# Unit 8's k transposed by VectorE and an HBM round trip, with new engine sequences, in an RWKV and ELU-MLP kernel on one Trainium2 core

## Chip, core and metric

The kernel runs on one core of one Trainium2 chip. The metric is the device time of one execution in microseconds (us), the median of several runs. All times below come from those runs or from one profiled execution of the same kernel.

## The reference, cut to what matters

```
B, H, S, D = 4, 8, 768, 48
state = zeros(B, H, D, D)
for t in range(S):
    cur = einsum('bhd,bhe->bhde', u * k[t], v[t])
    y[t] = einsum('bhd,bhde->bhe', r[t], state + cur)
    state = w[t][..., None] * state + einsum('bhd,bhe->bhde', k[t], v[t])
x = y as (B*S, H*D) = (3072, 384)
h = x @ w_in                        # 384 -> 2048
g = where(h > 0, h, exp(min(h, 0)) - 1)
out = g @ w_out                     # 2048 -> 384
```

A linear recurrence over 768 steps with a decay per channel (RWKV) feeds a two-layer perceptron with an ELU between its layers. All data are float32.

## The kernel before

**Work.** The recurrence is computed in chunks. There are 24 units: units 0 to 3 are one batch each over the first 128 steps, every later unit is two batches over 64 steps. Four units give the 512 columns of one of six blocks of the perceptron (c = 0 to 5). Each block runs over 16 slices of the hidden layer. A float32 product is made of three TensorE passes (w_h by x_h, w_h by x_l, w_l by x_h), so one slice is nine multiplications of 128x128 by 512 columns in layer one (`g1`, line 267) and nine in layer two (`g2`, line 298). Block 0 has 23 pieces (n = 0 to 22), since its columns are taken in halves at first, and each later block 16, so pieces go to n = 102.

**Steps of a unit i.** On VectorE (DVE): `es` and `gs` (decay products by scans, lines 461 and 470/471), `rkc` and then `rh` (k and r scaled, 495 and 476), `mk` (the upper triangle of the scores is put into the tile `ams`, 599 to 605), `sc` and `up` (the state, 632 and 698), `xl` (the low part of x, 690). On ScalarE (ACT): `md` (the diagonal, 504), `sp` (the diagonal spread into `ams`, 518, eight instructions for units 0 to 7; later units spread on GpSimd by an affine select, 529), `kt` (609), `xh` (686). On TensorE (PE): `pd` (500), `s` (scores, 570), `va` (for units from 8: the next unit's scores and this unit's state update, 570 and 640), `v` (values, 550). `mk` of unit i needs `s` and `sp` of unit i, `v` needs `mk`.

**Steps of a piece n.** g1 (PE), `r1` and `r2` (ACT, 271 and 274), `stt` (DVE, 277), `gh` (ACT, 281), `gl` (DVE, 285), g2 (PE). There are two PSUM buffers for g1's result, so g1 of n waits for `stt` of n - 2.

**Weights.** Every slice f is loaded raw (`raw`, 227), made float on ACT (`a`, 231) and DVE (`cc`, 235), split (`wh` on ACT, `wl` on DVE, 731), and its largest value is taken (`big`, DVE, 734), which is used at the end alone. Slices 0 and 1 are split later: `wt` (ACT), `wl` (DVE) and `wh` on GpSimd (POOL, line 727).

**The transpose of k.** `va` needs k with time on the partitions. For units 0 to 8 TensorE transposes (line 563, within `s`; for unit 8 a step of its own, `tr`), and ACT copies the result from PSUM (`kt`). For the units in TURN (9 to 21) VectorE transposes blocks of 32x32 (`tn`, 618), four DMAs write them to HBM in another order (`tw`, 623), and one DMA reads them back (`tk`, 627). Then the k load of the unit takes 128 rows, not 112.

**What sets the order.** Each of the five queues has its order written out in a table (SEQUENCE); each engine takes its steps strictly in that order. All loads, stores and copies are on one queue, that of SyncE (SP). A planner with a table of costs (COST) merges the five orders into one program text; within an engine it changes nothing. FILL puts warm-up multiplications by a matrix of ones (line 426) ahead of the named PE steps at the start; one call is two multiplications in the trace.

Of the kernel before, what the change touches and what calls it, by code (L numbers as in the profile page):

```python
# [85 lines left out]
g2.37 g2.38 g1.41 g1.42 g2.39 va.13 v.13 g2.40 g1.43 g2.41 g1.44 g1.45 g2.42 g2.43 g1.46 va.14 v.14 g1.47 g2.44 g2.45 g1.48 g1.49 va.15 v.15 g2.46
g1.50 g2.47 g2.48 g1.51 g1.52 g2.49 g2.50 g1.53 g1.54 va.16 v.16 g2.51 g1.55 g2.52 g1.56 g2.53 g2.54 va.17 v.17 g1.57 g1.58 g2.55 g1.59 g2.56 g2.57
va.18 v.18 g1.60 g1.61 g2.58 g1.62 g1.63 g2.59 g2.60 g1.64 g2.61 va.19 v.19 g1.65 g2.62 g1.66 g2.63 g1.67 g2.64 g1.68 g2.65 g1.69 g2.66 g1.70 g2.67
va.20 v.20 g1.71 g2.68 g1.72 g2.69 g2.70 g1.73 g1.74 g2.71 g1.75 g1.76 g2.72 g2.73 g2.74 va.21 v.21 g1.77 g2.75 g1.78 g1.79 g2.76 g1.80 va.22 v.22
# [5 lines left out]
es.0 gs.0 rkc.0 es.1 rh.0 gs.1 rkc.1 mk.0 rh.1 cc.0 es.2 rkc.2 gs.2 mk.1 rh.2 cc.1 es.3 stt.0 gs.3 cc.2 xl.0 stt.1 xl.1 wl.2 cc.3 rkc.3 stt.2 mk.2
rh.3 stt.3 wl.3 cc.4 es.4 es.5 gl.3 wl.4 cc.5 mk.3 stt.4 wl.5 stt.5 rk.4 gl.4 big.3 cc.6 stt.6 gs.4 gl.5 xl.3 gl.6 xl.2 rku.4 stt.7 md.4 stt.8 cc.7
wl.6 rh.4 stt.9 sc.4 rk.5 gl.9 cc.8 gs.5 rku.5 stt.10 md.5 stt.11 rh.5 wl.7 mk.4 wl.8 gl.11 gl.10 cc.9 sc.5 rk.6 stt.12 stt.13 xl.4 es.6 up.4 rku.6
gl.13 gl.12 cc.10 gs.6 mk.5 stt.14 wl.9 gl.14 rh.6 cc.11 stt.15 md.6 wl.10 rk.7 wl.11 cc.12 gl.15 stt.16 up.5 xl.5 rku.7 es.7 sc.6 cc.13 stt.17 wl.12
gl.16 mk.6 md.7 cc.14 gs.7 gl.17 sc.7 stt.18 rh.7 wl.13 stt.19 up.6 wl.14 es.9 gl.18 xl.6 cc.15 stt.20 es.8 gl.19 wl.15 rk.8 mk.7 sc.8 stt.21 gs.9
gl.20 gl.21 rk.9 rku.8 xl.7 gs.8 rku.9 rh.8 stt.22 md.8 md.9 rh.9 gl.22 up.7 stt.23 tn.9 es.10 rk.10 gl.23 sc.9 stt.24 gs.10 rh.10 gl.24 stt.25 tn.10  # L100
es.11 rk.11 gl.25 rku.11 mk.8 big.10 stt.27 stt.26 md.11 rku.10 md.10 up.8 gs.11 gl.27 gl.26 mk.9 sc.10 rh.11 es.12 stt.28 big.11 rk.12 gl.28 xl.8
stt.29 gs.12 big.2 stt.30 up.9 tn.11 mk.10 gl.29 sc.11 rh.12 stt.31 xl.9 es.13 gl.30 gl.31 wl.1 wl.0 rku.12 gs.13 md.12 es.14 rk.13 stt.32 gl.32
rku.13 up.10 stt.33 gs.14 gl.33 tn.12 stt.34 sc.12 rk.14 rh.13 xl.10 stt.35 mk.11 gl.34 md.13 rku.14 gl.35 es.15 big.9 tn.13 stt.36 mk.12 rh.14 gl.36
up.11 xl.11 stt.37 gs.15 md.14 es.16 rk.15 stt.38 sc.13 rku.15 gs.16 gl.38 gl.37 mk.13 md.15 tn.14 rh.15 up.12 stt.39 rk.16 stt.40 xl.12 gl.39 rku.16
tn.15 gl.40 stt.41 md.16 rh.16 es.18 gl.41 gs.18 up.13 stt.42 sc.14 stt.43 gl.42 es.17 gs.17 gl.43 tn.16 stt.44 big.12 mk.14 sc.15 big.14 stt.45 gl.44
xl.13 rk.17 rh.17 rku.17 gl.45 es.19 stt.46 mk.15 big.13 up.14 xl.14 big.6 tn.17 stt.47 big.0 gs.19 md.17 gl.46 rk.18 stt.48 gl.47 sc.16 rh.18 stt.49
gl.48 xl.15 es.20 tn.18 up.15 rku.18 stt.50 mk.16 md.18 rh.19 gl.49 sc.17 gl.50 rk.19 stt.51 stt.52 gl.51 gs.20 gl.52 rk.20 tn.19 rku.19 big.15 stt.53
md.19 es.21 gs.21 stt.54 up.16 gl.53 gl.54 big.5 big.4 mk.17 sc.18 rku.20 stt.56 xl.16 stt.55 mk.18 gl.55 gl.56 rh.20 big.8 rk.21 tn.20 rku.21 stt.57
stt.58 xl.17 rh.21 es.22 gl.57 es.23 up.17 stt.59 gl.58 up.18 gs.23 sc.19 md.20 gl.59 tn.21 md.21 stt.60 rk.22 stt.61 gl.60 stt.62 gs.22 big.7 gl.61
mk.19 rku.22 stt.63 xl.18 md.22 gl.62 rk.23 stt.64 rku.23 gl.63 md.23 stt.65 up.19 rh.22 sc.21 gl.64 sc.20 gl.65 stt.66 stt.67 xl.19 mk.20 gl.66 gl.67  # L110
big.1 stt.68 gl.68 stt.69 up.20 gl.69 stt.70 xl.20 mk.21 gl.70 sc.22 stt.71 gl.71 stt.72 gl.72 stt.73 stt.74 gl.73 gl.74 stt.76 rh.23 stt.75 gl.75
mk.22 gl.76 xl.21 stt.77 stt.78 up.21 gl.77 sc.23 gl.78 stt.79 least gl.79 stt.80 stt.81 gl.80 gl.81 mk.23 verdict stt.82 gl.82 xl.22 stt.84 stt.83
gl.84 gl.83 stt.85 xl.23 stt.86 gl.85 gl.86 stt.87 gl.87 stt.88 gl.88 stt.89 gl.89 stt.90 gl.90 stt.91 stt.92 gl.91 gl.92 stt.93 gl.93 stt.94 stt.95
gl.94 gl.95 stt.96 gl.96 stt.97 stt.98 gl.97 gl.98 stt.99 gl.99 stt.100 gl.100 stt.101 stt.102 gl.101 gl.102 end.1 end.2 end.3
# [1009 lines left out]
```

## Time and profile before

| | us |
|---|---|
| median of 3 runs | 486.15 (486.03 to 486.21) |
| the profiled execution | 486.13 |
| its span, first to last instruction | 484.4 |
| TensorE busy in the span | 475.7 (98%) |
| VectorE busy | 359.1 (74%) |
| ScalarE busy | 260.4 (54%) |
| GpSimd busy | 40.7 (8%) |

The span is 1.73 us shorter than the execution. Busy time of TensorE comes from multiplications whose ends are modelled, so a wait shows in the starts of the rows rather than in the busy share. The granted TensorE clock is 1.00 in the whole span.

### The profile page before, as it was taken

The numbers are of one execution on the slowest core, as the hardware profiler recorded it, in microseconds if no ns is written. First come the engines' busy times: TensorE is split into PE (matmuls) and PEld (weight loads), VectorE is DVE, ScalarE is ACT, GpSimd is POOL, SyncE is SP. The second block draws the span as 40 slices with busy tenths as digits, with TensorE's granted clock in tenths as the row PEclk, the third lists the DMA queues.
The fourth block names the chain that finished last, engine by engine and source line by source line (L and its number), as shares of the span: only waits on it lengthen the run. The fifth ranks groups of instructions, "written<-read, shape, count | busy, mean of one in ns | idle before, by whom it ended". The sixth has DMA issues, their size and how long they took to land.

```text
span 484.4 us, 12143 instructions
## 1 busy us (share of the span) xinstructions
PE 475.7 (98%) x4978; PEld 395.3 (82%) x4978; DVE 359.1 (74%) x545; ACT 260.4 (54%) x535; POOL 40.7 (8%) x56
## 2 busy tenths in 40 slices
...
GB/s 276 363 319 293 149 250 244 146 41 205 89 260 129 187 141 117 241 146 104 209 156 107 216 101 207 89 87 81 133 59 39 38 2 1 65 2 0 0 2 66
DMA packets 75418, 64.91 MB, mean 134 GB/s; under 512 B 56976, under 2 KB 57360, under 8 KB 75360
## 3 DMA queue, kind: packets, MB, share of 16 engines
q1 hardware_dynamic: 74784, 63.33, 46.3%
q8 instruction: 39, 0.64, 0.6%
...
## 4 chain that ended last, share of the span: by engine, by line
PE 75%; DVE 16%; issue 3%; DMA 3%; ACT 2%; DVEq 0%; POOL 0%; POOLq 0%
PE ph L267 32%; PE acc L298 31%; PE py L550 2%; PE px L570 2%; PE acc L426 2%; DVE ams L605 2%; DVE m L277 2%; PE px L550 2%; DVE gl L285 2%; DVE eg L461 2%; DMA w<-in_wkr_dram 1%; DVE k L476 1%; PE px L640 1%; DVE tops L734 1%; DMA k<-in_wkr_dram 1%
## 5 line engine op out<-in xcount | busy, mean ns | idle before, releaser
L271 ACT ACTIVATE m<-ph 128x512 f32<-128x512 f32 (+2 forms) x103 | 58.3, 567 | 102.0 <-PE ph L267 69.8
L267 PE MATMUL ph<-xh,w_l 128*128 128x512 f32 (+1 forms) x294 | 112.0, 381 | 0.0
L298 PE MATMUL acc<-gh,w_l 128*128 128x512 f32 (+1 forms) x292 | 111.2, 381 | 0.0
L277 DVE SCALAR_TENSOR_TENSOR m<-m,ph 128x512 f32<-128x512 f32 (+2 forms) x103 | 66.2, 646 | 57.2 <-ACT m L274 56.6
L281 ACT CAST gh<-m 128x512 fp32r<-128x512 f32 (+1 forms) x98 | 58.9, 602 | 86.6 <-PE acc L298 60.4
L267 PE MATMUL ph<-xh,w_h 128*128 128x512 f32 (+1 forms) x264 | 102.5, 388 | 1.8 <-DVE m L277 1.4
L298 PE MATMUL acc<-gh,w_h 128*128 128x512 f32 (+1 forms) x264 | 102.3, 388 | 0.0
L285 DVE TENSOR_TENSOR gl<-m,gh 128x512 fp32r<-128x512 f32 (+1 forms) x98 | 67.0, 690 | 46.3 <-ACT gh L281 45.1
L298 PE MATMUL acc<-gl,w_h 128*128 128x512 f32 (+1 forms) x264 | 100.4, 380 | 0.3 <-DVE gl L285 0.3
L267 PE MATMUL ph<-xl,w_h 128*128 128x512 f32 (+1 forms) x264 | 100.3, 380 | 0.0
L267 PEld LDWEIGHTS ph<-xh,w_l 128*128 128x128 f32 x294 | 55.3, 188 | 10.8
L298 PEld LDWEIGHTS acc<-gh,w_l 128*128 128x128 f32 x292 | 54.9, 188 | 10.5
L274 ACT ACTIVATE m<-m 128x512 f32<-128x512 f32 (+2 forms) x103 | 61.2, 601 | 1.7
L267 PEld LDWEIGHTS ph<-xh,w_h 128*128 128x128 f32 x264 | 49.6, 188 | 13.8 <-DVE m L277 3.3
L298 PEld LDWEIGHTS acc<-gh,w_h 128*128 128x128 f32 x264 | 49.6, 188 | 10.3
L298 PEld LDWEIGHTS acc<-gl,w_h 128*128 128x128 f32 x264 | 49.6, 188 | 9.7 <-DVE gl L285 0.7
L267 PEld LDWEIGHTS ph<-xl,w_h 128*128 128x128 f32 x264 | 49.7, 188 | 8.9
L529 POOL TENSOR_SCALAR_AFFINE_SELECT ams<-md 64x512 f32<-64x512 f32 x32 | 32.1, 1002 | 242.2 <-PE py L550 164.2
L461 DVE TENSOR_TENSOR_SCAN eg<-w,reset 112x520 f32<-112x520 f32 (+1 forms) x24 | 30.1, 1256 | 2.8 <-DMA w<-in_wkr_dram 2.8
L471 DVE TENSOR_TENSOR_SCAN eg<-w,reset 112x520 f32<-112x520 f32 (+1 forms) x24 | 30.3, 1263 | 0.8
L476 DVE TENSOR_TENSOR k<-k,eg 112x1024 f32<-112x1024 f32 x24 | 29.1, 1214 | 0.1
L605 DVE COPY_PREDICATED ams<-upper_h,px 64x512 f32<-64x512 uint32 x32 | 23.5, 735 | 1.4 <-PE px L570 0.9
...
## 6 DMA issues: line engine op xcount, KB each, us to landing
...
out_dram<-o SPq DMA_DIRECT2D x15, 256.0 KB, 4.0
rows<-turn SPq DMA_DIRECT2D x52, 64.0 KB, 2.8
```

The source lines that it names most:

```text
L267: nc.tensor.matmul(ph, w[f][:, 0, k], y[:, k], start=(k == n == 0), stop=(k == NK - 1 and n == 2))
L271: act(s["m"], s["ph"], AF.Relu, scale=-1.0)
L274: act(s["m"], s["m"], AF.Exp, scale=-1.0)
L277: stt_(s["m"], s["m"], -1.0, s["ph"], ALU.add, ALU.max)
L281: nc.scalar.copy(s["gh"], s["m"])
L285: nc.vector.tensor_tensor(s["gl"], s["m"], s["gh"].bitcast(F32), ALU.subtract)
L298: nc.tensor.matmul(a_, w[f][:, 1, m], fold(s, g[:, a:b]), start=(first and n == 0), stop=(final and n == 2))
L461: nc.vector.tensor_tensor_scan(out=eg[:, 0, 0:n][:, ::-1], data0=u_["w"][:, 1:n + 1][:, ::-1], data1=reset[:, 0, 0:n][:, ::-1], initial=0. ...
L471: nc.vector.tensor_tensor_scan(out=u_["eg"][:, 1, 1:n + 1], data0=u_["w"][:, 0:n], data1=reset[:, 1, 0:n], initial=0.0, op0=ALU.mult, op1= ...
L476: tt(t, t, u_["eg"][:, :, 0:u_["n"]].rearrange("d z (s t) -> d z s t", t=u_["L"] + 1)[..., 1:], ALU.mult)
L529: nc.gpsimd.affine_select(out=am[rs, h].rearrange("t q p s -> t (q p) s"), in_=u_["md"][rs].rearrange("t q p -> t (q p)").unsqueeze(2).bro ...
L605: nc.vector.copy_predicated(u_["am"][rs, h], above[L][rs], pa[rs])
```

## The change

TURN begins at 8: unit 8 loses `tr` on PE (four transposes) and `kt` on ACT, and gets `tn` on DVE, four DMAs `tw` and one DMA `tk` on SP. In the planner's table the duration of `tn` and the landing of `tk` are set to new values. The table of sequences is new for all five queues, and FILL has 45 calls where it had 36. What each step computes is as before.

```
-FILL = {("pd",0):17,("s",0):5,("pd",1):3,("s",1):2,("v",1):8,("s",2):1,("g2",0):0}
+FILL = {("pd",0):17,("s",0):5,("pd",1):4,("s",1):2,("v",0):3,("g1",0):3,("v",1):2,("g1",1):6,("g1",2):3,("g2",0):0}
-COST: tn=0.62
+COST: tn=0.703
-TURN = range(9, 22)
+TURN = range(8, 22)
-(PE) g2.18 s.7 g2.19 v.7 g1.22 g2.20 g1.23 g2.21 g1.24 tr.8 g2.22 g1.25 ...
+(PE) s.7 g1.21 v.7 g2.19 g1.22 g1.23 g2.20 g1.24 g2.21 g2.22 g1.25 ...
+(SP) ld_v.8 tc.8 ld_k.10 ld_w.10 tw.8 tc.9 store.0.2 ld_w.11 ld_rk.11 rc.8 ld_rk.10 tk.8
-  add(("tk", i), "SP", DMA_ISSUE, lambda u_=u_: turn_in(u_), [("tw", i)], size=K["dtk"], lands=0.6)
+  add(("tk", i), "SP", DMA_ISSUE, lambda u_=u_: turn_in(u_), [("tw", i)], size=K["dtk"], lands=1.8)
```

The first place is VectorE at the start, from `gs` of unit 1 to the triangle `mk` of unit 1 (`ams<-upper,acc`). Before:

```order
L470 RECIPROCAL reset<-eg 112x4
L471 SCALAR_TENSOR_TENSOR eg<-w,reset 112x516
L495 TENSOR_TENSOR rkc<-k 112x512
L599 COPY_PREDICATED ams<-upper,px 128x512 x2
L476 TENSOR_TENSOR k<-k,eg 112x1024
L235 SCALAR_TENSOR_TENSOR w_f<-wraw,top 128x768
L461 SCALAR_TENSOR_TENSOR eg<-w,reset 112x516
L495 TENSOR_TENSOR rkc<-k 112x512
L470 RECIPROCAL reset<-eg 112x4
L471 SCALAR_TENSOR_TENSOR eg<-w,reset 112x516
L599 COPY_PREDICATED ams<-upper,acc 128x512 x2
```

Now:

```order
L470 RECIPROCAL reset<-eg 112x4
L471 SCALAR_TENSOR_TENSOR eg<-w,reset 112x516
L476 TENSOR_TENSOR k<-k,eg 112x1024
L599 COPY_PREDICATED ams<-upper,px 128x512 x2
L235 SCALAR_TENSOR_TENSOR w_f<-wraw,top 128x768
L599 COPY_PREDICATED ams<-upper,acc 128x512 x2
L235 SCALAR_TENSOR_TENSOR w_f<-wraw,top 128x768
L495 TENSOR_TENSOR rkc<-k 112x512
L461 SCALAR_TENSOR_TENSOR eg<-w,reset 112x516
```

Unit 2's `es`, `rkc` and `gs` stood ahead of unit 1's triangle; now they follow it.

The second place is TensorE at the start, from `pd` of unit 1 to `v` of unit 1 (`acc<-ams,wide`). Before:

```order
L500 MATMUL py<-ubd,rkc 128x2 x4
L550 MATMUL px<-ams,wide 32x128 x16
L640 MATMUL px<-wide,kt 48x48 x8
L426 MATMUL acc<-ones 128x128 x2
L563 MATMUL py<-ident,k 128x112 x4
L570 MATMUL acc<-k 128x128 x8
L263 MATMUL ph<-wide,w_f 128x128 x3
L500 MATMUL py<-ubd,rkc 128x2 x4
L426 MATMUL acc<-ones 128x128 x8
L550 MATMUL acc<-ams,wide 32x128 x16
```

Now:

```order
L500 MATMUL py<-ubd,rkc 128x2 x4
L426 MATMUL acc<-ones 128x128 x2
L563 MATMUL py<-ident,k 128x112 x4
L570 MATMUL acc<-k 128x128 x8
L426 MATMUL acc<-ones 128x128 x3
L550 MATMUL px<-ams,wide 32x128 x16
L640 MATMUL px<-wide,kt 48x48 x8
L426 MATMUL acc<-ones 128x128 x3
L263 MATMUL ph<-wide,w_f 128x128 x3
L500 MATMUL py<-ubd,rkc 128x2 x4
L426 MATMUL acc<-ones 128x128 x2
L550 MATMUL acc<-ams,wide 32x128 x16
```

Unit 1's scores moved ahead of unit 0's values, and the warm-ups are spread over more places.

The third place is GpSimd from its clearing of the tile `wide` on; `w_g<-wt` are the two weight copies, and two affine selects make one unit's spread. Before:

```order
L387 MEMSET reset 112x1040
L388 MEMSET reset 112x8
L535 MEMSET wide 32x512 x3
L529 AFFINE_SELECT ams<-md 64x512 x10
L727 CAST w_g<-wt 128x768 x2
L529 AFFINE_SELECT ams<-md 64x512 x22
```

Now:

```order
L387 MEMSET reset 112x1040
L388 MEMSET reset 112x8
L535 MEMSET wide 32x512 x3
L529 AFFINE_SELECT ams<-md 64x512 x4
L727 CAST w_g<-wt 128x768 x2
L529 AFFINE_SELECT ams<-md 64x512 x28
```

The copies stood behind the spread of unit 12; now they stand behind that of unit 9.

## Rows read from the trace of the kernel before

**Rows 1.** The page, busy us and share of the span by engine.
```profile
PE 475.7 (98%) x4978; PEld 395.3 (82%) x4978; DVE 359.1 (74%) x545; ACT 260.4 (54%) x535; POOL 40.7 (8%) x56
```

**Rows 2.** Windows: stretch, its length, busy us by engine, clock, DMA share, GB/s.
```profile
0.00:45.00 45.00, 42.72 (x479) 38.99 (x480) 42.08 (x65) 34.33 (x89) 5.12 (x19) 1.00 0.94 322
45.00:125.00 80.00, 79.01 (x1118) 66.35 (x1117) 77.92 (x120) 59.01 (x128) 6.90 (x7) 1.00 0.55 167
125.00:250.00 125.00, 123.34 (x1513) 100.05 (x1512) 117.49 (x173) 56.78 (x114) 18.49 (x18) 1.00 0.64 165
```

**Rows 3.** Timeline of VectorE, 0 to 46 us: start, us, what, count, [idle before].
```profile
14.73 1.23 DVE L461 TENSOR_TENSOR_SCAN eg<-w,reset 112x516 f32<-112x516 f32 x1
...
32.79 2.37 DVE L461 TENSOR_TENSOR_SCAN eg<-w,reset 112x520 f32<-112x520 f32 x2
...
37.13 1.35 DVE L599 COPY_PREDICATED ams<-upper,px 128x512 f32<-128x512 uint32 x2
```

**Rows 4.** Timeline of ScalarE, 0 to 46 us: the spread of unit 1's diagonal.
```profile
13.24 2.46 ACT L518 ACTIVATE ams<-ident,md 128x128 f32<-128x128 f32 x8
```

**Rows 5.** Timeline of TensorE, 0 to 46 us.
```profile
11.28 0.94 PE L426 MATMUL acc<-ones 128*128 128x128 f32 x6
12.05 0.95 PE L500 MATMUL py<-ubd,rkc 112*128 112x2 f32 x8
...
38.54 1.08 PE L550 MATMUL px<-ams,wide 128*32 128x128 f32 x32 [0.72 <-DVE ams L599]
...
40.04 0.39 PE L267 MATMUL ph<-xh,w_h 128*128 128x256 f32 x1
```

**Rows 6.** Timeline of TensorE, unit 8's transposes; last, two pieces from the chain.
```profile
116.15 0.55 PE L563 MATMUL py<-ident,k 112*128 112x112 f32 x4
116.47 0.47 PE L298 MATMUL acc<-gh,w_h 128*128 128x512 f32 x1
116.78 0.39 PE L298 MATMUL acc<-gl,w_h 128*128 128x512 f32 x1
...
118.79 4.08 PE ph L267 x18
```

**Rows 7.** TensorE within v of unit 7, and the page's queue of instructions.
```profile
105.52 0.35 PE L550 MATMUL px<-k,st 48*32 48x64 f32 x17 [0.99 <-issue]
...
q8 instruction: 39, 0.64, 0.6%
```

**Rows 8.** Timeline of GpSimd, VectorE and TensorE around 163 us.
```profile
162.66 2.06 POOL L727 CAST w_g<-wt 128x768 fp32r<-128x768 f32 x2
...
162.70 1.33 DVE L285 TENSOR_TENSOR gl<-m,gh 128x512 fp32r<-128x512 f32 x1 [0.74 <-ACT gh L281]
163.95 1.18 DVE L486 TENSOR_TENSOR rk<-rk,ub 128x384 f32<-128x384 f32 x1
...
166.25 0.50 PE L267 MATMUL ph<-xh,w_h 128*128 128x512 f32 x1 [0.98 <-DVE m L277]
```

**Rows 9.** Waits: the weight loads' stops for VectorE's stt, us, times, longest.
```profile
PEld ph L267 <- DVE m L277: 3.3, 4, 1.4
```

**Rows 10.** Groups on VectorE by line: count | busy us, mean ns | idle before.
```profile
L285 DVE TENSOR_TENSOR gl<-m,gh 128x512 fp32r<-128x512 f32 (+1 forms) x98 | 67.0, 690 | 46.3 <-ACT gh L281 45.1
...
L471 DVE TENSOR_TENSOR_SCAN eg<-w,reset 112x520 f32<-112x520 f32 (+1 forms) x24 | 30.3, 1263 | 0.8
...
L734 DVE TENSOR_REDUCE tops<-w_h 128x1 f32<-128x768 f32 x14 | 13.1, 942 | 0.0
...
L698 DVE TENSOR_TENSOR st<-st,px 112x384 f32<-112x384 f32 x18 | 9.8, 543 | 1.9 <-PE px L640 1.8
L618 DVE STREAM_TRANSPOSE turn<-k 128x512 f32<-128x512 f32 x13 | 9.1, 702 | 0.0
```

**Rows 11.** The page's DMA issues: count, KB each, median us to landing.
```profile
rows<-turn SPq DMA_DIRECT2D x52, 64.0 KB, 2.8
turn<-rows SPq DMA_DIRECT2D x13, 256.0 KB, 4.2
```

More of the change, by code (lines that the diff above doesn't have):

```diff
@@ L86 @@
[L86 to L89, printed above, removed]
@@ L93 @@
+g2.101 g2.102
 """,
     DVE="""
[L95 to L114, printed above, removed]
+es.0 gs.0 rkc.0 rh.0 es.1 rkc.1 gs.1 rh.1 mk.0 cc.0 mk.1 cc.1 rkc.2 es.2 xl.0 gs.2 es.3 rh.2 stt.0 xl.1 cc.2 gs.3 stt.1 cc.3 rkc.3 wl.2 mk.2 big.2
@@ new lines @@
+cc.4 stt.2 wl.3 rh.3 cc.5 stt.3 big.3 gl.3 wl.4 mk.3 wl.5 stt.4 cc.6 gl.4 stt.5 es.4 xl.2 stt.6 xl.3 gl.5 rk.4 gl.6 cc.7 rku.4 stt.7 wl.6 sc.4 rk.5
+stt.8 md.4 gs.4 stt.9 rh.4 cc.8 rku.5 gl.9 es.5 stt.10 wl.7 stt.11 mk.4 gl.10 cc.9 gl.11 gs.5 wl.8 stt.12 md.5 wl.9 cc.10 stt.13 rk.6 es.6 gl.12 gl.13
+rh.5 stt.14 sc.5 up.4 cc.11 xl.4 stt.15 gl.14 wl.10 wl.11 gl.15 mk.5 cc.12 stt.16 gs.6 es.7 rku.6 gl.16 sc.6 md.6 rh.6 rk.7 xl.5 stt.17 rku.7 up.5
+cc.13 wl.12 sc.7 md.7 mk.6 stt.18 wl.13 gl.17 gs.7 cc.14 gl.18 rh.7 xl.6 up.6 stt.19 es.8 wl.14 gs.8 mk.7 gl.19 cc.15 stt.20 sc.8 wl.15 es.9 xl.7
@@ new lines @@
+stt.21 gl.20 rk.9 gl.21 gs.9 stt.22 up.7 rh.8 rku.9 tn.8 stt.23 gl.22 rk.8 sc.9 rku.8 md.8 stt.24 es.10 wl.1 gl.23 rh.9 md.9 gs.10 stt.25 gl.24 rh.10
+mk.8 gl.25 wl.0 tn.9 stt.26 es.11 gl.26 rk.10 stt.27 gs.11 rku.10 up.8 stt.28 md.10 rk.11 big.0 gl.27 es.12 rku.11 sc.10 gs.12 stt.29 tn.10 gl.28 mk.9
+xl.8 stt.30 md.11 gl.29 rh.11 mk.10 rh.12 gl.30 stt.31 es.14 tn.11 gl.31 stt.32 big.5 es.13 rk.12 up.9 gs.14 stt.33 gl.32 gs.13 gl.33 rku.12 stt.34
+rk.13 sc.11 gl.34 tn.12 rku.13 rh.13 xl.9 stt.35 md.13 es.15 gl.35 mk.11 md.12 up.10 stt.36 xl.10 gs.15 mk.12 gl.36 tn.13 up.11 big.11 stt.37 xl.11
@@ new lines @@
+sc.17 gl.53 rku.19 rku.20 up.16 stt.54 gl.54 mk.17 md.19 sc.18 stt.56 stt.55 gl.55 tn.19 es.21 gl.56 xl.16 stt.58 md.20 stt.57 big.15 gl.57 up.17
+gs.21 sc.19 rk.21 rku.21 md.21 rh.20 tn.20 gl.58 stt.59 gl.59 stt.60 rh.21 gl.60 rk.23 mk.18 stt.61 rku.23 stt.62 gl.61 es.23 stt.63 gl.62 rk.22 xl.17
+mk.19 up.18 rku.22 md.22 gl.63 stt.64 tn.21 gl.64 stt.65 xl.18 stt.66 gl.65 sc.20 big.4 mk.20 gs.23 gl.66 es.22 up.19 stt.67 gl.67 stt.68 xl.19 md.23
+stt.69 gl.69 gl.68 sc.21 up.20 gs.22 stt.70 gl.70 mk.21 stt.71 rh.22 xl.20 stt.72 gl.71 gl.72 stt.73 up.21 sc.22 rh.23 sc.23 gl.73 stt.74 xl.21 stt.75
@@ L115 @@
+gl.74 gl.75 mk.22 stt.76 gl.76 stt.77 gl.77 stt.78 mk.23 gl.78 stt.79 gl.79 stt.80 gl.80 stt.81 xl.22 stt.82 gl.81 gl.82 stt.83 gl.83 stt.84 stt.85
+xl.23 gl.84 gl.85 stt.86 gl.86 stt.87 stt.88 gl.87 least gl.88 stt.89 stt.90 gl.89 gl.90 verdict stt.91 gl.91 stt.92 gl.92 stt.93 gl.93 stt.94 gl.94
+stt.95 gl.95 stt.96 gl.96 stt.97 stt.98 gl.97 gl.98 stt.99 stt.100 gl.99 gl.100 stt.101 stt.102 gl.101 gl.102 end.1 end.2 end.3
 """,
     ACT="""
-md.0 pc.1 sp.0 pc.0 kt.0 a.0 md.1 sp.1 xf.0 up.0 kt.1 xh.0 r1.0 a.1 md.2 sp.2 r2.0 xf.1 a.2 r1.1 up.1 xh.1 r2.1 wh.2 a.3 pc.3 kt.2 r1.2 r2.2 pc.2 wh.3
```

80 lines of the change are left out of this document (44 added, 36 removed).

## The prediction

> **What bounds the kernel now.** I read the page first: TensorE is busy 98% of the span [rows 1], so the time is what TensorE has to do plus the places where it waits or fills in. The windows then say who makes it wait: up to 45 us VectorE is busy 42.08 of 45 us, up to 125 us 77.92 of 80, up to 250 us 117.49 of 125 [rows 2]. So there are two columns of work, both nearly full for half of the span, and after some 250 us TensorE alone counts. The clock is 1.00 in all of it [rows 2]; it has no term here. In the head TensorE's values of unit 3 wait 0.72 us for VectorE's triangle of that unit, and the piece behind them, g1.6, begins at 40.04 [rows 5]. From there on TensorE runs without a gap except at a few places: one stop of 0.99 us within `v` of unit 7 [rows 7], and four stops of its weight loads for VectorE's `stt`, 3.3 us together, the longest 1.4 [rows 9]. The longest of them has its cause in sight: at 162.66 GpSimd runs its two weight copies for 2.06 us, and in that time VectorE's gl takes 1.33 and its rk by u 1.18 [rows 8]; TensorE's next piece starts at 166.25 after 0.98 us of idle time [rows 8]. The sum is made on the profiled execution, 486.13 us, 0.02 below the median; its span is 484.4 and 1.73 lies around it. The end (partial sums, output) is not touched.
>
> **Unit 8.** TensorE's four transposes go. From their start to the next group's are 116.47 - 116.15 = 0.32 us, and that group takes 0.31 to its second multiplication where the steady step is 4.08 / 18 = 0.23: 0.08 more [rows 6]. They lie on a TensorE that is never idle there, so all of it counts: -0.4 us. ScalarE loses a copy that nothing waits for: 0. VectorE gets one block transpose of 0.70 [rows 10]; it is part of the column sums below. SP gets five issues, and the way from the transpose to k's rows is at least 2.8 + 4.2 = 7 us [rows 11]. In the new order `tn` comes two steps behind `rh` of unit 8, and between unit 8's `rh` and its `va` TensorE has some ten pieces of 2.04 us (nine steps of 0.23 [rows 6]) to do, so the 7 us have about twice their length of cover; what is queued on SP between `tw` and `tk` is a store, which waits for ScalarE's copy of block 0's result, three loads and unit 8's eight small copies. I take these as hidden, cost 0; if `tk` lands late, `va` of unit 8 waits one for one, and TensorE with it. The new durations in the planner's table change no engine's order beyond what the sequences show: 0. The k load of unit 8 has 128 rows for 112: hidden under its several us of lead.
>
> **The head: +1.0 us.** Now unit 1's triangle comes right behind `cc` of slice 0. In the trace the same ten steps that then stand ahead of it are done at 14.73, when `es` of unit 2 starts [rows 3]. But the triangle also needs unit 1's spread from ScalarE. That one starts at 13.24 and takes 2.46 [rows 4], and its start hangs on `pd` of unit 1, which stands behind four warm-ups instead of three: three took 12.05 - 11.28 = 0.77, so one is 0.26 [rows 5]. The spread then ends at 13.24 + 0.26 + 2.46 = 15.96, and VectorE stands idle from about 14.6 to 16.0: 1.4 us. Before, three steps of unit 2 lay in that hole. Up to unit 3's triangle the new order has two steps less (`es` of units 4 and 5, 2.37 us [rows 3]) and two `big` more (0.94 each [rows 10], 0.86 from start to start): -2.3 + 1.7. So unit 3's triangle starts at 37.13 + 1.4 - 0.6 = 37.9, plus some 0.2 for ScalarE's results that arrive just in time; `v` of unit 3 follows at once as it did before [rows 5], and g1.6 starts about 41.0 instead of 40.04 with the same TensorE work behind it. The warm-ups lie in time in which TensorE waits anyway: cost 0 beyond the one named. Bounds: -0.6 if the spread were on time, +1.5 if nothing of the hole is made good. I take +1.0, because the spread is a chain of rows with no slack in it.
>
> **The stop in unit 7: -1.0 us.** The stop of 0.99 us waits for nothing that the profile shows [rows 7]. It lies in the densest stretch: `v` of unit 7 is 128 multiplications with 128 weight loads. TensorE's instructions come by a queue of their own, 39 packets for 2 x 4978 multiplications and loads [rows 1, 7], one for about 255 of them, so `v` of unit 7 eats one packet by itself. Units 4 to 6 have the same 256 and no such stop; it depends on where a packet begins. Counted in the two programs, unit 7's `v` now stands 18 instructions later in the stream, with the same nine multiplications between its scores and itself; the packet is then asked for while these run (2 us) and not when the burst begins. I take the stop as gone; bounds 0 and -1.0. [...]
>
> **The later stops: -1.0 us.** Here the columns must be compared. Ahead of the `stt` that the stop at 166.25 waits for (n = 33), eleven steps of VectorE no longer stand that did (two `big`, one `gs`, one `gl`, seven small ones of 0.54 to 0.58), and four do instead (`tn` of unit 8, two `big`, one `gs`). With 0.94, 1.46 (a scan of 1.26 and its reciprocal), 0.69, 0.54 and 0.70 [rows 10] that is 7.9 against 4.0: 3.9 us less. Of these, 1.4 go to the hole of the head; and TensorE comes earlier itself by some 2.4 us, for `va` and `v` of unit 10 have moved behind that place and the transposes are gone. So the margin hardly grows. At n = 47 (the stop around 234) the same count gives 7.7 against 5.0, less the 1.4: VectorE is 1.3 us earlier and TensorE 0.4. The copies on GpSimd now come three units earlier; what they add on VectorE, 1.33 + 1.18 less the usual 0.69 and 0.55 or some 1.3 us [rows 8, 10], stays in the column. [...] Bounds for all four stops: -3.3 if every one goes, +1.3 if the copies make a new one and the old ones stay. I take -1.0, by the 1.3 of n = 47, less some new small stops.
>
> **Sum:** 486.13 - 0.4 + 1.0 - 1.0 - 1.0 = 484.7 us, 0.3% below before.
>
> **The rivals.**
> 1. *The margins are eaten by the hole of the head*: VectorE is late by the 1.4 us, the four stops come back at other pieces with 3.3 us in all, and only unit 7's stop and the transposes go: 486.13 + 1.0 - 0.4 - 1.0 = 485.7. [...] For it: VectorE's 117.49 of 125 us. I give both together 27%.
> 2. *Slower: VectorE's column is the bound up to 200 us.* The hole (1.4) and the copies (1.3) both come ahead of the stretch from 140 to 170 us in the new order, where `va` of units 9 and 10 stand later and VectorE's steps lie closer to TensorE's need. From the point where VectorE is over 3 us behind its place, each further us stops TensorE: 486.13 + 1.0 - 0.4 + 1.3 = 488.0 with unit 7's stop kept, 487.0 without; 487.4 between them. Against it: 3.9 us less work ahead of n = 33. 17%.
> 3. *The stops go altogether*: 486.13 + 1.0 - 0.4 - 1.0 - 3.3 = 482.4, or 482.9 with some rest. For it: ahead of n = 39 VectorE's steps are fewer by more still. 10%.
> 4. *The round trip does not arrive*: unit 8's `tk` waits on SP behind the store; at 3 us late it would cancel the gain (487). Its lead speaks against it; it is within rival 2's share.
>
> **How the numbers follow.** The forecast has 46%, the rivals 27, 17 and 10. A measurement of this kernel tells 0.2% (0.97 us) from no change, so faster means below 485.18. The forecast's own range is 484.0 to 485.6: four fifths of it are faster, 0.37, with rival 3 and a few hundredths of rival 1 0.50; same 0.32 (the rest of the forecast and most of rival 1); slower 0.18. The range for 8 in 10 leaves out a tenth at each side: from 482.9, rival 3's value, to 487.4, the middle of rival 2.
>
> **What would show it.** In the trace after: the triangle of unit 1 starting near 16.0 with an idle gap of about 1.4 ahead of it, behind ScalarE's spread; unit 3's triangle near 38.1 and g1.6 near 41.0; no transposes (line 563) after unit 7's; `va` of unit 8 without a wait for the tile `turn`; no idle time within `v` of unit 7; the sum of the weight loads' waits for `stt` near 2.3 us instead of 3.3; the two copies near 125 to 130 us with a stretched `gl` beside them. I am wrong if g1.6 is not later than before, if `v` of unit 7 still stops, or if the waits for VectorE are above 3.3 us.

## The result: 0.7% slower, and the profile after

The changed kernel takes 488.15 us (median of 11 runs, 486.00 to 491.03) where the kernel before takes 485.80 beside it: a ratio of 1.0069, 95% interval 1.0051 to 1.0086. (Ratios, here and below, are taken over all runs; the two medians alone give 1.0048.) Forecast were 484.7, so the sign is wrong. The profiled execution takes 488.15 us, its span is 486.4 (484.4 before). Busy time by engine, share of the span and instructions, after:

```profile
PE 477.7 (98%) x4992; PEld 399.0 (82%) x4992; DVE 359.9 (74%) x546; ACT 259.6 (53%) x534; POOL 39.3 (8%) x56
```

TensorE is busy 2.0 us longer than in [rows 1]. As it hardly works more, the longer time must lie in a few places, and the granted clock says which. Windows of after: stretch, length, busy us of PE, PEld, DVE, ACT, POOL, clock, DMA share, GB/s.

```profile
98.00:102.00 4.00, 4.00 (x79) 2.94 (x77) 3.97 (x6) 2.82 (x5) 0.00 (x0) 1.00 1.02 334
102.00:106.00 4.00, 1.55 (x112) 1.31 (x117) 3.22 (x5) 2.37 (x4) 0.00 (x0) 0.99 0.56 152
106.00:110.00 4.00, 4.00 (x36) 3.12 (x36) 2.22 (x4) 1.31 (x3) 0.00 (x0) 0.58 0.58 158
```

In the second TensorE is busy 1.55 of 4 us; in the third it is busy throughout, at a mean clock of 0.58. Before, the clock was 1.00 in every stretch [rows 2]. The first shows DMA queues that are full (1.02, 334 GB/s) just ahead of the place. The timeline of TensorE there, after (start, us, instruction, count, idle before and its releaser):

```profile
102.52 0.80 PE L550 MATMUL px<-ams,wide 64*32 64x64 f32 x60
...
105.93 0.66 PE L550 MATMUL px<-k,st 48*32 48x64 f32 x26 [2.45 <-issue]
106.52 0.79 PE L298 MATMUL acc<-gh,w_h 128*128 128x512 f32 x1
107.11 0.63 PE L298 MATMUL acc<-gl,w_h 128*128 128x512 f32 x1
107.53 0.63 PE L298 MATMUL acc<-gh,w_l 128*128 128x512 f32 x1
...
109.52 0.39 PE L298 MATMUL acc<-gl,w_h 128*128 128x512 f32 x1
...
109.98 0.40 PE L267 MATMUL ph<-xh,w_h 128*128 128x512 f32 x1
```

The stop within `v` of unit 7, 0.99 us before [rows 7], is 2.45 us now. Behind it the multiplications of g2.19 come 0.42 us apart (107.53 - 107.11) and not 0.23: TensorE has a lower clock there, right after it stood idle. The window of that stretch, columns as above, has a granted clock of 0.50:

```profile
105.92:109.33 3.41, 3.40 (x33) 2.65 (x33) 2.17 (x4) 1.31 (x3) 0.00 (x0) 0.50 0.61 153
```

g2.19 takes 109.98 - 106.52 = 3.46 us, and a piece behind a `v` at full clock takes 2.18 (105.80 to 107.98 in the trace before).

Now the balance, by the starts of pieces up to which both orders have run the same steps on TensorE. g1.6 begins 1.00 later (41.04; 40.04 in [rows 5]). g1.22 begins at 109.98 where it began at 105.80:

```profile
105.80 0.50 PE L267 MATMUL ph<-xh,w_h 128*128 128x512 f32 x1
```

That is 4.18 later, so between the two 3.18 are lost, 1.46 by the longer stop and 1.4 by the clock; 0.3 is not placed. TensorE's last group of multiplications (six of 128 columns) begins 1.07 later, so 3.1 us are won back behind g1.22. Its first, before and after:

```profile
479.95 0.22 PE L298 MATMUL py<-gh,w_g 128*128 128x128 f32 x1
481.02 0.22 PE L298 MATMUL py<-gh,w_g 128*128 128x128 f32 x1
```

From there to the end of the span it takes 5.41 where it took 4.47; 1.07 + 0.94 gives the 2.0 of the spans. That last stretch is the same code in both. What takes longer in it are the last stores of the output, which ScalarE issues and not SP; the first two of them, KB each and us to landing, before and after:

```profile
out_dram<-o ACTq DMA_DIRECT2D x2, 256.0 KB, 2.1
out_dram<-o ACTq DMA_DIRECT2D x2, 256.0 KB, 3.3
```

It goes with the instructions, which come by DMA too (40 packets on queue q8, 0.66 MB, in this profile). In the five profiles of this study in which a 40th packet of them begins within 0.6 us of that last group (at 481.01 here; the changed kernel and its four versions with the same warm-up), the stretch takes 5.41 to 6.31 us; in the other nine it takes 4.47 to 5.05. That the packet makes it longer is argued from this; no run tests it.

The later stops are nearly gone. Waits of after (us, times, longest):

```profile
PEld ph L267 <- DVE m L277: 0.5, 1, 0.5
```

0.5 us of waiting for `stt` against 3.3 in [rows 9].

### The profile page after: what moved, and what is told of

Same layout as the page of the kernel before. It is cut to its first block, busy times and chain, and to the rows that moved or that the text cites. A ratio compares the mean times of both kernels' runs of the same rounds, so it can differ in the third digit from the quotient of the medians.

```text
span 486.4 us, 12166 instructions
## 1 busy us (share of the span) xinstructions
PE 477.7 (98%) x4992; PEld 399.0 (82%) x4992; DVE 359.9 (74%) x546; ACT 259.6 (53%) x534; POOL 39.3 (8%) x56
## 4 chain that ended last, share of the span: by engine, by line
PE 96%; DVE 2%; issue 1%; ACT 1%; DMA 0%; POOL 0%; DVEq 0%; ACTq 0%; POOLq 0%
PE acc L298 39%; PE ph L267 39%; PE py L550 3%; PE px L570 3%; PE acc L426 3%; PE px L550 2%; PE px L640 2%; PE acc L295 1%; PE ph L263 1%; PE py L500 1%; PE py L563 1%; DMA wide<-st 0%; DVE gl L285 0%; DVE m L277 0%; DVE eg L461 0%
## 5 line engine op out<-in xcount | busy, mean ns | idle before, releaser
L529 POOL TENSOR_SCALAR_AFFINE_SELECT ams<-md 64x512 f32<-64x512 f32 x32 | 30.2, 944 | 229.8 <-PE py L550 119.3
L476 DVE TENSOR_TENSOR k<-k,eg 112x1024 f32<-112x1024 f32 x24 | 30.4, 1265 | 0.9 <-issue 0.8
L461 DVE TENSOR_TENSOR_SCAN eg<-w,reset 112x520 f32<-112x520 f32 (+1 forms) x24 | 29.5, 1234 | 1.2 <-DMA w<-in_wkr_dram 1.2
L471 DVE TENSOR_TENSOR_SCAN eg<-w,reset 112x520 f32<-112x520 f32 (+1 forms) x24 | 29.8, 1240 | 0.8
```

Source lines behind the costliest of these rows:

```text
L461: nc.vector.tensor_tensor_scan(out=eg[:, 0, 0:n][:, ::-1], data0=u_["w"][:, 1:n + 1][:, ::-1], data1=reset[:, 0, 0:n][:, ::-1], initial=0. ...
L471: nc.vector.tensor_tensor_scan(out=u_["eg"][:, 1, 1:n + 1], data0=u_["w"][:, 0:n], data1=reset[:, 1, 0:n], initial=0.0, op0=ALU.mult, op1= ...
L476: tt(t, t, u_["eg"][:, :, 0:u_["n"]].rearrange("d z (s t) -> d z s t", t=u_["L"] + 1)[..., 1:], ALU.mult)
L529: nc.gpsimd.affine_select(out=am[rs, h].rearrange("t q p s -> t (q p) s"), in_=u_["md"][rs].rearrange("t q p -> t (q p)").unsqueeze(2).bro ...
```

## What the stop waits for: an instruction packet behind loads

Instructions come by DMA, on queues that the profile names. The line of the larger one, before, stands in [rows 7]; after, it is (packets, MB, share of 16 engines):

```profile
q8 instruction: 40, 0.66, 0.6%
```

That is 16 KB to a packet. That q8 is TensorE's queue is an estimate from the counts: 39 packets for 2 x 4978 multiplications and weight loads before and 40 for 2 x 4992 after, one for about 250 to 255 of them. The place in the stream where one packet ends is called a border here. In the trace after, the packet ahead of the stop begins at 103.44 and lasts to 104.68; TensorE goes on at 105.93. Before, the packet began at 102.88 and TensorE went on at 105.52. So from the packet's start to the next instruction there are 2.5 to 2.6 us in both, and what differs is the start. The DMA view of after, from 99.0 to 103.4 (packets, MB, share of 16 engines):

```profile
q1 hardware_dynamic: 538, 1.38, 104.2%
```

and from 103.4 to 104.7:

```profile
q1 hardware_dynamic: 61, 0.07, 19.6%
q8 instruction: 1, 0.02, 6.0%
```

The packet begins when the data run out. Before there were no data in that stretch at all (2 GB/s from 99.0 to 102.8), and still a stop of 0.99. `v` of unit 7 takes its 256 instructions (128 multiplications and as many loads) in 1.63 us where it has no stop (106.55 to 108.18 in the first experiment below), less than the 2.5 from a packet's start to the next instruction, so a packet that starts late shows there at once. But why this one started late is open. Three further profiles have the same order on TensorE up to the piece behind unit 7's scores and no data there either (the kernel before with the border later, and twice with unit 8 alone; all below). In them the packet starts at 101.45, 101.22 and 101.26, and `v` of unit 7 has no stop. Its end in one of the versions with unit 8 alone, 30 multiplications in a row:

```profile
103.98 0.54 PE L549 MATMUL px<-k,st 48*32 48x64 f32 x30
```

Counted from the start of the piece behind unit 7's scores, the packet starts after 0.57 to 0.82 us in these three, after 2.14 in the kernel before and after 3.69 in the changed kernel. So the kernel before has some 1.4 us of delay without data, which nothing here explains, and the changed kernel some 3 us.

In the changed kernel the data are a burst of loads that SP issued after `ld_v.9`, which stands at the head of its queue until unit 6's values are done and `wide` is free. SP's timeline of after:

```profile
91.78 0.49 SPq L448 DMA_DIRECT2D wide<-in_vp_dram  x1
92.32 0.59 SPq L451 DMA_DIRECT2D wide<-in_vp_dram  x1
...
96.68 1.11 SPq L448 DMA_DIRECT2D wide<-in_vp_dram  x2
```

Theory 1, the fetch theory: the packet is late because it queues behind those loads, and TensorE reaches its border too soon. Theory 2: only the place in the instruction stream counts. Theory 3: `v` of unit 7 waits for something of its own.

## Experiments on the stop

**Other times for the loads.** SP of the changed kernel:

```
-ld_v.9 ld_v.7 raw.15 ld_k.8 ld_w.9 ld_k.9 ld_rk.9 ld_v.8 tc.8
+ld_v.7 raw.15 ld_k.8 ld_v.8 ld_w.9 ld_k.9 ld_rk.9 tc.8 ld_v.9
```

> The changed kernel, with SP's order ahead of unit 7's values altered: the load of unit 9's v (which waits there for unit 6's values and holds up everything behind it) goes behind unit 8's four state copies, and the load of unit 8's v goes three places forward, so that the loads no longer land all together from 95 to 105 us. Nothing else is altered. Theory 1 (instruction packet behind data): TensorE's packet of instructions is asked for as usual, near 100 us, but waits some 3 us for the DMA queues, which move 334 GB/s there; with the loads gone from that place the packet starts near 100.5 and not at 103.44, the stop within v of unit 7 falls from 2.45 us to under 0.5, the granted clock stays at 1.00, and the median falls from 488.15 to about 484.5 (2.45 of stop and some 1.4 of low clock less). Theory 2 (place in the stream alone): the packet's delay has nothing to do with the loads; stop 2.45 and median 488 as they are. Theory 3 (v of unit 7 waits for something of its own): as theory 2.

Measured: 487.39 us, 1.0039 of before (1.0023 to 1.0056). The stop in `v` of unit 7 is gone, as theory 1 said, but the gain is not there: the stop has moved. TensorE of this kernel, unit 6's values, and unit 7's:

```profile
91.27 0.72 PE L550 MATMUL px<-ams,wide 64*32 64x64 f32 x48
94.37 0.35 PE L550 MATMUL px<-ams,wide 64*32 64x64 f32 x16 [2.38 <-issue]
...
107.05 0.80 PE L550 MATMUL px<-ams,wide 64*32 64x64 f32 x60
107.63 0.24 PE L550 MATMUL px<-k,st 48*32 48x64 f32 x1
```

The loads now run from 88 to 92.5, where the packet for unit 6's values is wanted; it begins at 91.92, and 2.45 us later TensorE goes on. The clock falls there too (0.62 from 95 to 99 us): the next piece takes 3.50 us. So with the stream untouched, the stop sits at the loads: theory 1 holds against 2 and 3. In unit 7's values the packet now starts at 104.63, with no data on the queues, 0.35 us after the piece behind the scores began.

**Half a megabyte less in the burst.**

```
-ld_v.9 ld_v.7 raw.15 ld_k.8 ld_w.9 ld_k.9 ld_rk.9 ld_v.8 tc.8
+ld_v.7 ld_v.8 ld_v.9 raw.15 ld_k.8 ld_w.9 ld_k.9 ld_rk.9 tc.8
```

> The changed kernel, with two loads alone moved on SP: v of unit 7 (256 KB) and v of unit 8 (two of 128 KB) go ahead of unit 9's v, which waits for unit 6's values; so half a megabyte less lands between 92 and 105 us, and none of it from 87 to 91 us, where the packet for v of unit 6 is asked for. The fetch theory: the rest lands by some 101 us, the packet for v of unit 7 starts at 100.5 to 101.5, no stop over 0.5 us in v of unit 6 or 7, no low clock, median about 483.5 to 484.5 (488.15 less 2.45 of stop, 1.4 of low clock). If a packet is late whenever the queues are busy at any time in the 4 us ahead of it, a stop of 0.5 to 1.5 us is left, median 485. If the loads have nothing to do with it: 488.

Measured: 485.28 us, 1.0005 (0.9996 to 1.0014). The packet begins at 101.58, again as the data end (its view from 101.0 to 102.7):

```profile
q1 hardware_dynamic: 107, 0.27, 41.7%
q8 instruction: 1, 0.02, 4.1%
```

TensorE there:

```profile
103.88 0.43 PE L550 MATMUL px<-k,st 48*32 48x64 f32 x26 [0.34 <-issue]
104.24 0.50 PE L298 MATMUL acc<-gh,w_h 128*128 128x512 f32 x1
104.58 0.39 PE L298 MATMUL acc<-gl,w_h 128*128 128x512 f32 x1
```

0.34 us in place of 2.45, and the next multiplications 0.34 and 0.23 apart, as behind unit 7's values in the kernel before, where the granted clock is 1.00. Two loads moved ahead are worth 2.9 us of the median. The stop is the one that the fetch theory gave (under 0.5 us); the median is the 485 that was expected with a stop of 0.5 to 1.5 us, and the spread of the runs (484.25 to 486.45) is not explained by this profile.

**TensorE later at the border.**

```
-s.7 g1.21 v.7 g2.19
+s.7 g1.21 g2.19 v.7
```

> The changed kernel, with one piece more between unit 7's scores and values on TensorE: s.7 g1.21 g2.19 v.7 for s.7 g1.21 v.7 g2.19. Theory 1: the packet starts at the same 103.4 and TensorE could go on at 105.9, but comes to that place only 2.05 us later, near 105.3: a stop of 0.6 us is left in place of 2.45, no low clock behind it, median about 485 (1.85 and 1.4 less than 488.15). Theory 2 in the form that v's 256 instructions always outrun a packet that is asked for when v begins: the stop stays at 2.4, median 488. Theory 3: the stop stays too, or moves with whatever v waits for. If the low clock comes with the length of the stop, it is gone here as well; if it comes with the place, it stays.

Measured: 485.53 us, 1.0011 (0.9996 to 1.0026). Unit 7's values:

```profile
105.89 0.24 PE L549 MATMUL px<-ams,wide 64*32 64x64 f32 x2 [0.76 <-issue]
```

The packet starts at 103.20 and TensorE goes on at 105.89, as in the changed kernel, but it has 2.05 us more work first: 0.76 us of stop, and no low clock behind it (the next multiplications start at 106.39, 106.72 and 106.95).

**Both.** The two edits together.

> The loads as in a_quiet, and g2.19 ahead of v of unit 7 on TensorE (as in a_later): 2 us more for the packet. The fetch theory: no stop in any run, no low clock, and the runs lie close together, median 483.2 to 483.8. If what spreads the changed kernel's runs is something else than these packets, they spread as in a_later (484.0 to 488.0).

Measured: 484.20 us, 0.9980 (0.9970 to 0.9990): faster than before, but less than expected. No stop in any `v` of the profiled run. The runs still spread, from 483.24 to 485.64, so these stops alone do not make the spread; the profiled one is of the long ones (485.30) and has 1.34 us in which TensorE's weight loads wait for the first `rkc` at 8 us, and 6.3 us from the last group of multiplications to the end, neither of which the edits touch.

**Another place in the stream.** `SMALL` calls are multiplications of 32x32.

```
-FILL = {("pd",0):17, ...
+FILL = {("pd",0):9, ...
+SMALL = {("pd",0):40}
```

> The changed kernel with 128 TensorE instructions more in the first warm-up (8 calls of the 17 become 40 small ones on a 32x32 corner), so that every later instruction stands half a packet later in the stream; the head should start at the same time within about 1 us. Theory 1 and 2 (a packet's border inside v of unit 7): the border moves to the 77th of v's 256 instructions, and the 256 ahead of it take 7.1 us in place of 3.9, so the stop in v of unit 7 goes; in its place the worst border comes right behind unit 4's values, in g2.11, whose 256 instructions take 1.9 us: a new stop there of 1.7 to 4.3 us near 63 us, with a low clock behind it if it is over 2; median 486 to 489. Theory 3: the stop stays in v of unit 7 and none appears behind unit 4's values; median 488.

Measured: 483.73 us, 0.9976 (0.9968 to 0.9985), the fastest version here although its head is 0.5 us later than that of the changed kernel. No stop in unit 7's values:

```profile
103.02 0.80 PE L556 MATMUL px<-ams,wide 64*32 64x64 f32 x60
103.61 0.24 PE L556 MATMUL px<-k,st 48*32 48x64 f32 x1
...
104.15 0.50 PE L299 MATMUL acc<-gh,w_h 128*128 128x512 f32 x1
```

The stop that was forecast for g2.11 did not come (that piece takes 1.18 us, as in the changed kernel). A packet began at 60.01 there, before `v` of unit 4 did, earlier than a count of some 255 to a packet allows. So the place in the stream counts as well as the loads, but where a packet is asked for is not settled, and I could not have chosen the shift by counting. Not all of the gain is the stop's: behind the last group of multiplications this version takes 4.73 us, 0.7 less than the changed kernel, and its 40th packet comes earlier, at 469.86.

**The same shift, with a shorter warm-up** (6 full, 43 small calls).

> As the run that shifts the stream by 128 instructions, but with 6 full and 43 small calls in the first warm-up (the same 128 instructions more), so that it ends at about 7.3 us and not 8.15. The fetch theory: the stream stands as there, no stop in v of unit 7, and the 0.5 us by which that kernel's head was later than the changed kernel's is won back: g1.6 near 40.9 to 41.0, median 483.73 - 0.5 = 483.2. If the head is set by VectorE alone and not by the warm-up, no gain: 483.7.

Measured: 484.14 us, 0.9972 (0.9959 to 0.9985). In the profiled run (483.08) g1.6 begins at 41.01 (41.54 in the shifted version), so the 0.5 us was won there; over the runs (483.02 to 485.56) it does not show.

**The kernel before, with the border later.**

```
-s.7 g2.19 v.7 g1.22 g2.20
+s.7 g2.19 g1.22 v.7 g2.20
```

> The kernel before, with one piece more between unit 7's scores and values on TensorE: s.7 g2.19 g1.22 v.7 for s.7 g2.19 v.7 g1.22. Theory 1: its stop of 0.99 us is the same kind; the packet comes at the same time and TensorE 2.05 us later, so the stop goes and the median falls from 485.8 to about 484.8. Theory 2: stop and median stay. Theory 3: the stop stays or moves.

Measured: 485.35 us, 1.0004 (0.9996 to 1.0013). There is no stop in its unit 7, but no gain either. In this profile the packet starts at 101.45 and not at 102.88, so by the 2.6 us from a packet's start there would have been no stop in the old order either. The 33 runs of the kernel before beside it say more: 25 lie between 484.7 and 485.3, eight between 485.9 and 486.5 (in another set of 31 runs, five lie between the two). The three runs of the prediction and the profiled one were all of the upper kind. This version has 11 of 12 runs at 485.0 to 485.8. That the upper kind is the one with the stop is argued, not shown, as only one run of each kernel has a profile. For it speak the distance of the two kinds, some 1 us, and the three profiles with the same order up to there in which the packet came early enough.

## Experiments on the other terms

**Unit 8 put back**, on the shifted version: TURN from 9, `tr` of unit 8 ahead of its scores on PE, `kt` behind `r2` of piece 25 on ACT, no `tn`, `tw`, `tk` of unit 8.

> As the run that shifts the stream by 128 instructions, with unit 8's transposes back on TensorE (TURN from 9): tr of unit 8 ahead of its scores, its copy on ScalarE behind r2 of piece 25, and no tn, tw, tk of unit 8. The prediction's term for unit 8 (0.4 us on TensorE, the round trip hidden): 0.4 more than that run, 484.1 against 483.73, with the two transposes' rows 0.3 to 0.4 us apart and no wait near them. Rival: the round trip costs as much elsewhere as it saves on TensorE: 483.7, no difference.

Measured: 484.91 us, 0.9997 (0.9985 to 1.0009). TensorE:

```profile
121.13 0.55 PE L568 MATMUL py<-ident,k 112*128 112x112 f32 x4
121.61 0.69 PE L575 MATMUL px<-k 48*64 48x64 f32 x32
```

The transposes take 121.61 - 121.13 = 0.48 us, and from g1.22 to `va` of unit 8 it is 27.90 us against 27.47 without them: 0.43. The term of the prediction was right. The medians are 1.2 apart, the profiled runs 1.3; of that, 0.5 is in the head (g1.6 at 42.08 for 41.54, behind a wait of unit 0's values that this edit does not touch) and 0.3 behind the last group of multiplications, so the median says no more than the sign.

**Unit 8 alone, in the order of before**, twice.

```
-(PE) g1.24 tr.8 g2.22      (ACT) kt.8 out.0.0
+(PE) g1.24 g2.22           (ACT) out.0.0
-(DVE) rh.8 stt.22 ... stt.23 tn.9 es.10 rk.10 gl.23
+(DVE) rh.8 tn.8 stt.22 ... stt.23 es.10 rk.10 tn.9 gl.23
-(SP) ld_k.10 ld_w.10 ld_rk.10 ld_v.9 ld_rk.11 tw.9 rc.8
+(SP) ld_k.10 tw.8 ld_w.10 ld_rk.10 ld_v.9 ld_rk.11 tk.8 rc.8 tw.9    (first)
+(SP) ld_k.10 ld_w.10 ld_rk.10 tw.8 ld_v.9 ld_rk.11 tk.8 rc.8 tw.9    (second)
```

> The kernel before with unit 8's transpose alone changed: TURN from 8, TensorE's tr and ScalarE's kt of unit 8 gone, tn of unit 8 behind its rh on VectorE (tn of unit 9 two steps later), its four tw and one tk on SP ahead of rc of unit 8; all other orders as before. The prediction's term: 0.4 us less, hidden otherwise, so a median of 484.6 against 485.04. Rival: the five issues hold up rc and tc of units 8 and 9 on SP by some 3 us and the tile turn holds up tn of unit 9, so va of unit 8 waits: 485 to 488, with a wait of TensorE's line 570 for a DMA or VectorE near 130 us.

Measured: 487.64 us, 1.0037 (1.0025 to 1.0050). That is the rival's time, but in another place: `va` of unit 8 does not wait. SP's four issues `tw`, which stand ahead of a load of `w`, delay that load. VectorE, and TensorE behind it:

```profile
116.86 1.24 DVE L460 TENSOR_TENSOR_SCAN eg<-w,reset 112x520 f32<-112x520 f32 x1 [2.24 <-DMA w<-in_wkr_dram]
```

```profile
121.42 0.50 PE L266 MATMUL ph<-xh,w_h 128*128 128x512 f32 x1 [2.40 <-DVE m L276]
...
122.03 0.63 PE L266 MATMUL ph<-xh,w_l 128*128 128x512 f32 x1
122.46 0.63 PE L266 MATMUL ph<-xh,w_h 128*128 128x512 f32 x1
```

Here the idle time has quite another cause, data, and the clock falls behind it as well (0.43 apart; 0.90 is granted from 110 to 125 us).

> As b_unit8, with unit 8's four tw behind the loads of unit 10's w and rk on SP in place of ahead of them. In b_unit8 VectorE's es of unit 10 waited 2.24 us for that load of w and TensorE's g1.26 then 2.8 us for stt. If the place on SP made that loss: no such wait, and the median is 484.6 to 485.1 (the kernel before's 485.04 less up to 0.4). If the round trip itself costs that much in the order of before: 487 again.

Measured: 486.24 us, 1.0026 (1.0016 to 1.0035). The wait for `w` is gone, but not all of the loss. VectorE of this one, unit 10's transpose:

```profile
124.16 0.71 DVE L617 STREAM_TRANSPOSE turn<-k 128x512 f32<-128x512 f32 x1 [1.01 <-DMA rows<-turn]
```

There is one tile `turn`, and with one unit more in the row its writer waits for the DMA that reads it. So the round trip is not free as such: it is free in the changed kernel's order, where SP and VectorE leave room for it, and costs some 1 us in the order of before. That this one wait makes all of it is not shown: TensorE's idle time behind it is 0.33 us, at unit 9's scores, and from g1.23 to g1.33 it takes 47.77 us where it took 46.79.

**The weight copies put back** near their old place, on the shifted version: `wl.1 wl.0` behind `gl.31`, `big.0` behind `gl.34` (DVE), `wh.1 wh.0` behind `sp.11` (POOL). In the kernel before, `big.0` stood behind `stt.47` and `wh.1 wh.0` behind `sp.12`.

> As the run that shifts the stream by 128 instructions, but with the two weight copies of GpSimd (and VectorE's two wl and one big for them) put back to where the kernel before has them: behind unit 11's spread, near 157 to 160 us, and not near 129. If the copies' place made the stops of TensorE for stt that the changed order no longer has, they come back near 160 to 170 us (1 to 1.4 us in one stop) and the median goes up by 1 to 1.5 to about 485. If the smaller column of VectorE ahead of n = 33 did it, as counted in the prediction (3.9 us less), the copies are absorbed: at most 0.3 us, 483.7 to 484.

Measured: 485.18 us, 0.9990 (0.9981 to 1.0000): 1.45 us more than the shifted version. The stops are back at 163.55 and 189.06:

```profile
163.55 0.50 PE L268 MATMUL ph<-xh,w_h 128*128 128x512 f32 x1 [0.52 <-DVE m L278]
```

and the waits of this kernel:

```profile
PEld ph L268 <- DVE m L278: 2.2, 4, 0.9
```

From `va` of unit 9 to that of unit 12 TensorE takes 49.13 us, without the move back 47.65: 1.48 of the gain hangs on where the copies run. In the changed kernel they run apart, and beside another instruction than `gl` (GpSimd, VectorE):

```profile
129.26 1.69 POOL L727 CAST w_g<-wt 128x768 fp32r<-128x768 f32 x1
133.36 0.83 POOL L727 CAST w_g<-wt 128x768 fp32r<-128x768 f32 x1 [2.41 <-DVE w_l L731]
```

```profile
128.60 1.67 DVE L476 TENSOR_TENSOR k<-k,eg 112x1024 f32<-112x1024 f32 x1
```

This `rh` takes 1.67 us where others take 1.22; nobody on TensorE's path waits for it. The stretch goes with the copy (0.45 us here), and it matters which instruction it hits: with the copies put back, at 157.30 to 159.47, the `stt` and the `big` beside them take 0.68 and 0.94 us, as elsewhere.

**The hole in the head filled**, on the version with the shorter warm-up.

```
-(DVE) mk.0 cc.0 mk.1 cc.1 rkc.2 es.2 xl.0
+(DVE) mk.0 cc.0 es.2 mk.1 cc.1 xl.0 rkc.2
-(SP) raw.0 raw.1 ld_v.0 ld_k.2 ld_w.2 ld_v.1
+(SP) raw.0 ld_v.0 ld_w.2 raw.1 ld_k.2 ld_v.1
```

> As a_short, and unit 2's es goes ahead of unit 1's triangle on VectorE, into the hole in which it waits for TensorE's scores and ScalarE's spread of unit 1; so that its data are there, SP loads w of unit 2 ahead of slice 1 and of k of unit 2, and rkc of unit 2 goes behind xl of unit 0. The theory of the head (VectorE's column up to unit 3's triangle, with 0.7 to 1.0 us of holes around unit 1's triangle, sets g1.6): the holes are filled, unit 3's triangle and g1.6 come 0.5 to 0.9 us earlier than in a_short, median 482.4 to 482.8. Rival: slice 1 or k of unit 2 then come late and open the same hole one step later: no gain, 483.2, or up to 0.5 slower.

Measured: 486.11 us, 1.0016 (1.0000 to 1.0032). The rival, and worse: slice 1 lands later, and the steps behind it wait. VectorE:

```profile
18.87 0.96 DVE L236 SCALAR_TENSOR_TENSOR w_f<-wraw,top 128x768 uint32<-128x768 uint32 x1 [1.37 <-ACT top L232]
```

g1.6 begins at 44.90, 3.9 us later than without the edit. Windows of this kernel, columns as above:

```profile
18.00:22.00 4.00, 1.89 (x15) 1.54 (x15) 2.88 (x5) 2.46 (x6) 0.00 (x0) 1.00 1.04 332
22.00:26.00 4.00, 4.00 (x57) 3.21 (x57) 3.04 (x4) 3.56 (x12) 0.00 (x0) 0.57 1.03 276
```

TensorE waits two times (0.91 and 1.20 us) and the low clock follows. The hole is filled; the loads are the scarcer thing there.

## Why the prediction was wrong, point by point

**The step that failed: "the stop in unit 7: -1.0".** It took the stop for a packet border and concluded from 18 instructions and from nine multiplications ahead of `v` that the packet would come in time. The first half holds: the stop ends some 2.5 us (2.30 to 2.69) after a packet's start in every profile that has it. The second does not: where no data were on the queues and no stop came, the packet starts 0.35 to 0.82 us after those nine multiplications begin, and in the changed kernel it starts after 3.69. The working counted instructions only and never asked what else is on the DMA queues when the packet is asked for. SP's order was in the diff: `ld_v.9` stood behind `tc.8` before and stands ahead of seven loads now; nine issues from 91.78 us on became one burst, whose data run up to 103.4 us. With the loads moved, the stop moves with them. The stop grew by 1.46 and brought 1.4 of low clock, +2.9 where -1.0 was written; that is 3.9 us and more than the whole miss of 3.45 against the forecast of 484.7. Why the kernel before had its 0.99 us stays open: by the three profiles without it, the place in the stream, on which the step relied, does not decide it alone.

Most packets cost TensorE no such stop. In the changed kernel there are 40, and its multiplications have one stop that waits for nothing in the profile (us, times, longest):

```profile
PE px L550 <- issue: 2.5, 1, 2.5
```

This one is 2.45 us, two of the versions have 2.38 and 0.76, and at unit 7's border it is gone when the data move.

**The clock.** "It has no term here" was read from [rows 2], in a trace whose longest wait on the way is 1.4 us [rows 9]. In the changed kernel it is a term of 1.4 us: behind stops of 2.45, 2.38 and 2.40 us most of TensorE's multiplications in the next piece came 0.42 to 0.43 us apart (granted clock 0.50 in the first of the three), behind single stops of 0.99, 0.98 and 0.76 they came 0.23 apart, the first step aside (granted clock 1.00 in the first two); behind two stops close together, 0.91 and 1.20, the clock was 0.57. The single runs of the changed kernel go the same way: the granted clock of the span is 0.999 at 486.00 us, 0.998 at 486.66, 0.995 to 0.997 at 487.6 to 488.4, and 0.991 to 0.992 at 490.7 to 491.0. The longest runs would fit two low stretches; that is argued.

**Unit 8: right**, 0.43 to 0.48 us by the rows, and hidden in this order.

**The head: right in sum, 41.04 for 41.0, not in its parts.** ScalarE and VectorE of after:

```profile
13.51 2.45 ACT L518 ACTIVATE ams<-ident,md 128x128 f32<-128x128 f32 x8
```

```profile
15.41 1.37 DVE L599 COPY_PREDICATED ams<-upper,acc 128x512 f32<-128x512 uint32 x2 [0.25 <-PE acc L570]
16.97 0.96 DVE L235 SCALAR_TENSOR_TENSOR w_f<-wraw,top 128x768 uint32<-128x768 uint32 x1 [0.19 <-ACT top L231]
...
37.98 1.38 DVE L599 COPY_PREDICATED ams<-upper,px 128x512 f32<-128x512 uint32 x2
```

The spread ends at 15.96 as worked out, but the triangle's first half starts before that, at 15.41, on TensorE's scores. The 1.4 us hole is 0.25 there, 0.19 and 0.28 at two later `cc`, and 0.41 at the first k load, 1.1 us in all. Unit 3's triangle is 0.85 late, forecast 0.8 to 1.0.

**The later stops: right sign, a third of the size.** Forecast 3.3 to 2.3; measured 3.3 to 0.5. The step said that what the copies add "stays in the column". It does, but more than half of what was won does not come from a shorter column: 1.5 of 2.8 us come back when the copies, with the `wl` that feed them, go back to their place.

**The base.** The sum stood on 486.13 us, which passed for the median. Over more runs that median is 485.0, and the profiled run is one of its longer ones. By the same terms the forecast would have been 1.1 us lower and the miss larger. And if the shorter runs are those without the stop, as argued above, the -1.0 had nothing to take away in most runs.

**The end: put at nothing.** "The end (partial sums, output) is not touched" is true of the code; in the profiled runs the stretch behind the last group of multiplications grew by 0.94 us, as described above.

**The rivals.** The slower one had its price near (487.4), but by another mechanism: VectorE's column, which costs 0.5 us of waiting in all. That the stop could grow was not among the rivals.
